# Block 1's standard deviation on ScalarE, block 2's statistics beside it, and the d mask later: a spectral mixer with a token MLP

## The chip, the cores and the metric

The kernel runs on one core of a Trainium2 chip. A core has five engines that run side by side and meet through semaphores: TensorE (PE) for matrix products, VectorE (DVE) and ScalarE (ACT) for element-wise work, GpSimd (POOL) for small operations and gathers, and SyncE (SP), whose queue issues most transfers (DMAs) between main memory and the core. Each engine works through its own list of instructions in order: an instruction that waits holds up all that stand behind it on that engine. The metric is the device time of one execution in microseconds (us), the median over several executions.

## The reference

Two branches work on the same 2048 tokens of 512 channels and are mixed by a gate per token.

```
g = sigmoid((x * gate_w).sum(-1, keepdims=True))
a = irfft2(rfft2(x) * (w_r + 1j*w_i))              # spectral branch, over tokens and channels
h = layernorm(x_B)                                 # over the channels
u = gelu(einsum("bsd,sf->bdf", h, w1) + b1)        # token MLP, 2048 -> 1792
b = transpose(einsum("bdf,fs->bds", u, w2) + b2)   # 1792 -> 2048
out = g * a + (1 - g) * b
```

The kernel takes one tensor x for both branches (`A_x`). All inputs and the output are bf16.

## The kernel before, in words

The 2048 tokens are 16 blocks of 128. The MLP's first product contracts over tokens, so it takes one block after another: `mm1(b, ft)` multiplies the weights of block b for one slice of 128 hidden features with the normalized block `hn[:, b]` and accumulates in PSUM. Eight feature slices (ft 0 to 7) are accumulated at the same time, so every block feeds eight matmuls of 512 columns, and PE can begin with block 0 as soon as that block is normalized. Blocks 0 to 11 go through in this order; then each slice takes blocks 12 to 15 and is passed to a gelu. The six other slices (`products`, line 459, weights `w1b`) and the whole second product (line 469, weights `w2t`) come later, as filling work between the matmuls of the spectral branch.

The front of the kernel is therefore a pipeline. SP's queue loads tokens (`load_x`, line 90, tiles `xa` and `xb`) and weights (`load_w1a`, line 93) in small pieces and in turn. DVE makes the statistics of a block (`bstat`, line 246) and aggregates them (line 253, or 297 for block 0). Then there are three ways to the normalized block:

- Block 0: ACT takes the square root of the variance plus epsilon (line 298), DVE the reciprocal (line 300) and the normalization (line 271). ACT needs its table for square roots for this, loaded by line 289; the later sines need another table, loaded by line 306.
- Blocks 1 to 5 (`NDVE` is 6): DVE adds epsilon (line 255), POOL raises to the power -0.5 (line 258), DVE normalizes (line 271).
- Blocks 6 to 15, in pairs: POOL makes the power; mean times that is formed on DVE (line 264, pairs 6/7 and 14/15) or POOL (line 262, the others); ACT normalizes (line 267).

DVE's order is written out by hand (the schedule is manual): the statistics of the next block stand between epsilon and the normalization of this block.

Beside this, the kernel makes the matrices of its Fourier transforms. DVE makes integer angles `md` for the d axis (line 291) and reduces them with a bit mask (line 195, function `mask`); ACT takes sines and cosines of them into `TD` (`sines_d`, lines 198 and 201). The same happens for the token axis: `ma`, `mc` made by ACT (lines 308 and 309), masked by DVE, sines into `TA`. SP's queue later transposes TD and TA into TI and TB (lines 347 and 349).

After that the spectral branch runs on DVE and PE: sums and differences of token blocks on DVE (`YA`, `YB`), token transforms (lines 514 to 518) and d transforms (line 526) on PE, the spectral weights on DVE (`PMA` and `PMB`, lines 533 to 563), the inverse on PE (lines 652 to 674, evacuated by ACT in line 630), and the last sums on DVE. Where PE's transforms stand among the filling matmuls is decided when the program is built, by a planner: `clock` starts at a given time and moves on by 0.2165 us for each filling matmul, and `fill_to(T)` issues filling matmuls until `clock` reaches a written due time (`T_TA`, `T_TB`, `T_IA`, `T_IB`, `T_Y`). The finished y blocks of the second product are evacuated by ACT (line 449).

Of the kernel before, what the change touches and what calls it, by code (L numbers as in the profile page):

```python
# [8 lines left out]
ActF = mybir.ActivationFunctionType  # L9
# [11 lines left out]
NFT = 14  # L21
FT1 = 8
NDVE = 6
# [20 lines left out]
def kernel(  # L44
# [13 lines left out]
    nc = tc.nc  # L58
# [9 lines left out]
    def H(i, shape, name, dt=BF16):  # L68
        return big.tile(shape, dt, tag=f"h{i}", name=name)
# [7 lines left out]
    def bank(name):  # L77
        return psum.tile([P, 512], F32, tag="mm", name=name, bufs=2)
# [10 lines left out]
    def load_x(b0, b1):  # L89
        nc.sync.dma_start(out=xh[b0 // 8][:, b0 % 8:(b1 - 1) % 8 + 1], in_=xv[:, b0:b1])  # L90

    def load_w1a(b0, b1):
        nc.sync.dma_start(out=w1a[b0 // 4][:, b0 % 4:(b1 - 1) % 4 + 1], in_=w1v[:, b0:b1, 0:FT1 * P])
# [28 lines left out]
    load_w1a(0, 1)  # L122
    load_x(1, 2)
    for b in range(1, 3):
        load_w1a(b, b + 1)
        load_x(b + 1, b + 2)
    load_x(4, 6)
    load_w1a(3, 4)
    load_x(6, 8)
# [16 lines left out]
    consts = small.tile([P, 6], F32, name="consts")  # L146
# [47 lines left out]
    def mask(m, n):  # L194
        nc.vector.tensor_single_scalar(m, m, n - 1, op=Alu.bitwise_and)

    def nsin(dst, m, n):
        nc.scalar.activation(dst, m, ActF.Sin, bias=c_mpi, scale=2.0 * PI_IN / n)

    def psin(dst, m, n):  # L200
        nc.scalar.activation(dst, m, ActF.Sin, bias=c_pi, scale=-2.0 * PI_IN / n)

    md = H(6, [P, 2, 3, P], "md", I32)
# [3 lines left out]
    def sines_d():  # L207
        nsin(TD[:, :, 1], md[:, 1], 1024)
        nsin(TD[:, :, 2], md[:, 0], 1024)
        psin(TD[:, :, 0], md[:, 0], 1024)  # L210

    def angles_a(v):
        mask(ma[v][:], 2048)
        if v == 0:
            mask(mc[:], 2048)

    def sines_a(v):
        if v == 1:
            nsin(TA[:, :, 1], ma[1][:], 2048)
        else:  # L220
            nsin(TA[:, :, 2], ma[0][:], 2048)
            psin(TA[:, :, 0], ma[0][:], 2048)
            nsin(TA[:, 0, 2, 0:1], mc[:], 2048)
            psin(TA[:, 0, 0, 0:1], mc[:], 2048)


    stats = small.tile([P, NB, nc.vector.BN_STATS_DIM], F32, name="stats")
    mv = small.tile([P, NB, nc.vector.BN_AGGR_DIM], F32, name="mv")
    rstd = small.tile([P, NB], F32, name="rstd")
# [6 lines left out]
    pb = bank("pb")  # L236
# [8 lines left out]
    def bstat(b):  # L245
        nc.vector.bn_stats(out=stats[:, b, :], in_=xh[b // 8][:, b % 8, :])  # L246

    def on_dve(b):
        return b <= NDVE or b == NB - 2

    def aggr(b0, b1):
        for b in range(b0, b1):
            nc.vector.bn_aggr(out=mv[:, b, :], in_=stats[:, b, :])
        eng = nc.vector if on_dve(b0) else nc.gpsimd
        eng.tensor_scalar(mv[:, b0:b1, 1], mv[:, b0:b1, 1], 1e-5, 0.0, op0=Alu.add, op1=Alu.add)  # L255
        if not on_dve(b0):
            nc.gpsimd.tensor_scalar(nmr[:, b0:b1], mv[:, b0:b1, 0], -1.0, 0.0, op0=Alu.mult, op1=Alu.add)
        nc.gpsimd.tensor_tensor(rstd[:, b0:b1], mv[:, b0:b1, 1], c_mhalf.to_broadcast([P, b1 - b0]), op=Alu.pow)  # L258

    def norm(b0, b1):  # L260
        if not on_dve(b0):
            nc.gpsimd.tensor_mul(nmr[:, b0:b1], nmr[:, b0:b1], rstd[:, b0:b1])  # L262
        else:
            nc.vector.scalar_tensor_tensor(nmr[:, b0:b1], mv[:, b0:b1, 0], -1.0, rstd[:, b0:b1],
                                           op0=Alu.mult, op1=Alu.mult)
        for b in range(b0, b1):
            nc.scalar.activation(hn[:, b, :], xh[b // 8][:, b % 8, :], ActF.Identity,  # L267
                                 bias=nmr[:, b:b + 1], scale=rstd[:, b:b + 1])

    def norm_dve(b):  # L270
        nc.vector.tensor_scalar(hn[:, b, :], xh[0][:, b, :], mv[:, b, 0:1], rstd[:, b:b + 1],  # L271
                                op0=Alu.subtract, op1=Alu.mult)
# [20 lines left out]

    bcol = small.tile([P, NFT + NB], F32, name="bcol")
    b1f, b2f = bcol[:, 0:NFT], bcol[:, NFT:]
    bstat(0)
    nc.vector.bn_aggr(out=mv[:, 0, :], in_=stats[:, 0, :])
    nc.scalar.activation(rstd[:, 0:1], mv[:, 0, 1:2], ActF.Sqrt, bias=consts[:, 5:6], scale=1.0)
    nc.scalar.copy(b1f, pb[:, 0:NFT])
    nc.vector.reciprocal(rstd[:, 0:1], rstd[:, 0:1])  # L300
    norm_dve(0)
    bstat(1)
    aggr(1, 2)
    norm_dve(1)
    bstat(2)
    nc.scalar.activation(sink[:], consts[:, 2:3], ActF.Sin, bias=c_mpi, scale=0.0)
    for v in range(2):
        nc.scalar.activation(ma[v][:], krow[:], ActF.Identity, bias=consts[:, 3 + v:4 + v], scale=acol[:, 0:1])
# [4 lines left out]
    for b in range(2, NDVE):  # L313
        bstat(b + 1)
        norm_dve(b)
        if b == 2:
            mask(md[:], 1024)
            sines_d()
        if b + 1 < NDVE:
            aggr(b + 1, b + 2)  # L320
    for b in range(NDVE, NB, 2):
        if b > NDVE:
            bstat(b)
        if b == NDVE + 2:
            norm(b - 2, b)
        bstat(b + 1)
        aggr(b, b + 2)
        if b == NB - 2:
            angles_a(1)
        if b > NDVE:  # L330
            norm(b, b + 2)
        if b == NB - 6:
            angles_a(0)
            sines_a(0)
# [4 lines left out]
    for q in range(4):  # L339
# [8 lines left out]
                                in_=TD[:].rearrange("p s t k -> p (s t k)"))  # L348
    nc.sync.dma_start_transpose(out=TB[:].rearrange("p s t k -> p (s t) k"),
                                in_=TA[:].rearrange("p s t k -> p (s t k)"))  # L350
# [132 lines left out]
    def hook(b):  # L483
        store(b)

    clock = [32.8]
    act = [0.0]

    def fill(n):
# [306 lines left out]
    b = NB - 1  # L796
# [36 lines left out]
```

## Time and profile before

| what | value |
|---|---|
| median of 3 runs | 129.39 us (129.38 to 129.5) |
| the profiled execution, own time | 129.24 us |
| its span, first to last instruction | 127.5 us |
| PE busy | 121.4 us, 95% |
| DVE busy | 111.5 us, 87% |
| ACT busy | 89.5 us, 70% |
| POOL busy | 40.9 us, 32% |
| granted TensorE clock | 0.999 |
| chain that ended last, by engine | PE 81%, DVE 6%, ACT 4%, POOL 3%, DMA 2%, issue 1% |
| moved by DMA | 24.05 MB |

The span covers only the instructions; the execution's own time is 1.74 us longer. A row of the time order gives start, duration, engine, line, operation, the tile written and the tiles read, and in brackets the idle time just before it with what ended it. The chain that ended last is found by going back from the last instruction, at each step to what released it. "busy" says how long an engine worked, not whether its work was on the path that sets the end.

### The profile page before, as it was taken

To read this page: it belongs to the slowest core of one execution; us is meant where nothing else is said; L and a number is where in the kernel's file an instruction comes from. 1 tells how busy PE (TensorE), PEld (TensorE's weight loads), DVE (VectorE), ACT (ScalarE), POOL (GpSimd) and SP (SyncE) were. 2 spreads that over 40 slices of the span, in tenths; PEclk is the share of its full clock that TensorE was granted. 3 is DMA by queue.
4 is the path that set the end of the run, shared out by engine and by line. 5 is a ranking of instruction groups with operands and counts; after the bars stand their busy time and mean duration, and the time that the engine had idled before them with its cause. 6 is when DMAs were issued, how large, how long until landed. Compare 5 with 4: busy or idle time off the path is not lost.

```text
span 127.5 us, 2061 instructions
## 1 busy us (share of the span) xinstructions
PE 121.4 (95%) x737; PEld 65.1 (51%) x750; DVE 111.5 (87%) x190; ACT 89.5 (70%) x136; POOL 40.9 (32%) x68
## 2 busy tenths in 40 slices
PE   6989999999999999999999999999999999999980
PEld 2334434444444576557764766467644444444570
DVE  4699998999999999999999999999999999992140
ACT  4774159999897799999994599339785599422410
POOL 7314378999843699300140000000000000250300
PEclk9999999999999999999999999999999999999999
DMA  3899999997899999999689205810021101279991
GB/s 100 279 314 367 375 377 351 292 309 249 206 224 161 306 290 292 291 278 296 153 234 292 50 0 154 261 42 0 0 75 53 41 5 49 72 86 197 184 211 29
DMA packets 34635, 24.05 MB, mean 189 GB/s; under 512 B 5536, under 2 KB 32032, under 8 KB 34624
## 3 DMA queue, kind: packets, MB, share of 16 engines
q1 hardware_dynamic: 32516, 21.02, 60.6%
q0 software_dynamic: 1936, 2.76, 12.5%
q8 instruction: 6, 0.10, 0.3%
q10 hardware_dynamic: 172, 0.13, 0.3%
q14 instruction: 5, 0.04, 0.1%
HBM read 19.15 MB, written 3.67 MB: 179 GB/s over the span
## 4 chain that ended last, share of the span: by engine, by line
PE 81%; DVE 6%; ACT 4%; POOL 3%; DMA 2%; issue 1%
PE yb L469 34%; PE u L459 16%; PE u L275 14%; PE ivt L658 4%; PE dp L526 3%; POOL rstd L258 3%; PE tok L517 3%; PE yb L801 2%; PE tok L518 2%; PE ivd L674 2%; DVE stats L246 2%; DVE hn L271 2%; DMA xa<-in_A_x_dram 2%; ACT R L630 2%; DVE mv L255 1%
## 5 line engine op out<-in xcount | busy, mean ns | idle before, releaser
L469 PE MATMUL yb<-gl,w2t 128*128 128x512 bf16 x203 | 46.4, 379 | 0.4
L469 PEld LDWEIGHTS <-w2t 128*128 128x128 bf16 x210 | 20.2, 98 | 22.0
L275 PE MATMUL u<-hn,w1a 128*128 128x512 bf16 x126 | 28.3, 379 | 0.9 <-DVE hn L271 0.4
L459 PE MATMUL u<-hn,w1b 128*128 128x512 bf16 x92 | 22.6, 379 | 0.2
L449 ACT ACTIVATE tbv<-yb,ombb,omg 128x512 bf16<-128x512 f32 x15 | 11.7, 778 | 13.5 <-PE yb L469 13.5
L275 PEld LDWEIGHTS <-w1a 128*128 128x128 bf16 x128 | 12.5, 98 | 16.6 <-issue 2.2
L779 POOL DMA_DIRECT2D out_dram<-ap x3 | 4.0, 1528 | 49.5 <-DVE ap L774 45.3
L459 PEld LDWEIGHTS <-w1b 128*128 128x128 bf16 x96 | 9.0, 98 | 8.0
L630 ACT CAST R<-ivt 128x1024 bf16<-128x1024 f32 x8 | 7.8, 1037 | 4.9 <-PE ivt L658 4.9
L286 ACT ACTIVATE junk<-prod 128x512 bf16<-128x512 bf16 x16 | 10.1, 630 | 0.3
L355 ACT ACTIVATE gl<-u,bcol 128x512 bf16<-128x512 f32 x14 | 9.2, 688 | 1.3 <-PE u L459 0.8
L258 POOL TENSOR_TENSOR rstd<-mv,consts 128x1 f32<-128x1 f32 (+1 forms) x10 | 6.7, 666 | 8.2 <-DVE mv L255 8.1
L630 ACT CAST H<-ivd 128x1024 bf16<-128x1024 f32 x7 | 6.8, 1026 | 0.8 <-PE ivd L674 0.8
L267 ACT ACTIVATE hn<-xb,nmr,rstd 128x512 bf16<-128x512 bf16 x8 | 5.9, 802 | 1.3 <-POOL nmr L262 1.3
L788 DVE TENSOR_TENSOR tbv<-tbv,ap 128x512 bf16<-128x512 bf16 x3 | 1.3, 426 | 5.6 <-ACT tbv L449 5.6
L246 DVE BATCH_NORM_STATS2 stats<-xa 128x6 f32<-128x512 bf16 x8 | 5.5, 686 | 0.4 <-DMA xa<-in_A_x_dram 0.4
L548 DVE TENSOR_TENSOR tatb<-PMA,wn 128x1024 bf16<-128x1024 bf16 x8 | 5.0, 690 | 0.2 <-PE tok L518 0.2
L246 DVE BATCH_NORM_STATS2 stats<-xb 128x6 f32<-128x512 bf16 x8 | 5.2, 676 | 0.0
L674 PEld LDWEIGHTS <-R 128*128 128x128 bf16 x64 | 3.9, 98 | 2.2 <-ACT R L630 2.2
L548 DVE TENSOR_TENSOR tatb<-PMB,wn 128x2048 bf16<-128x2048 bf16 x4 | 4.7, 1227 | 0.2
L674 PE MATMUL ivd<-TI,R 128*128 128x128 bf16 x64 | 4.9, 219 | 0.0
L519 ACT CAST ZA<-tok 128x1024 bf16<-128x1024 f32 x4 | 4.0, 1018 | 1.2 <-PE tok L518 1.1
(198 smaller groups left out, 222.7 us busy)
## 6 DMA issues: line engine op xcount, KB each, us to landing
w2t<-in_B_w_dram SPq DMA_DIRECT2D x8, 896.0 KB
w1b<-in_B_w_dram SPq DMA_DIRECT2D x3, 1024.0 KB
w1a<-in_B_w_dram SPq DMA_DIRECT2D x2, 1024.0 KB
out_dram<-tbv SPq DMA_DIRECT2D x14, 128.0 KB
out_dram<-ap POOLq DMA_DIRECT2D x3, 512.0 KB, 6.9
w1a<-in_B_w_dram SPq DMA_DIRECT2D x4, 256.0 KB
w1a<-in_B_w_dram SPq DMA_DIRECT2D x2, 512.0 KB
xb<-in_A_x_dram SPq DMA_DIRECT2D x2, 512.0 KB
```

What stands on the lines that cost most here:

```text
L246: nc.vector.bn_stats(out=stats[:, b, :], in_=xh[b // 8][:, b % 8, :])
L258: nc.gpsimd.tensor_tensor(rstd[:, b0:b1], mv[:, b0:b1, 1], c_mhalf.to_broadcast([P, b1 - b0]), op=Alu.pow)
L267: nc.scalar.activation(hn[:, b, :], xh[b // 8][:, b % 8, :], ActF.Identity, bias=nmr[:, b:b + 1], scale=rstd[:, b:b + 1])
L275: nc.tensor.matmul(u1[ft], lhsT=w1a[b // 4][:, b % 4, ft * P:(ft + 1) * P], rhs=hn[:, b, :], start=(b == 0), stop=(b == NB - 1))
L286: nc.scalar.activation(junk[:], prod[b // 8][:, b % 8], ActF.Copy, accum_out=glog[:, b:b + 1])
L355: nc.scalar.activation(gl[:, ft, :], src, ActF.Gelu_apprx_tanh, bias=b1f[:, ft:ft + 1], scale=1.0)
L449: nc.scalar.activation(tbv[0][:, b], y[:], ActF.Identity, bias=gate["ombb2"][:, b:b + 1], scale=gate["omg"][:, b:b + 1])
L459: nc.tensor.matmul(u[:], lhsT=w1b[c][:, b, k * P:(k + 1) * P], rhs=hn[:, b, :], start=(b == 0), stop=(b == NB - 1))
L469: nc.tensor.matmul(y[:], lhsT=w2t[b // 2][:, ft, (b % 2) * P:(b % 2 + 1) * P], rhs=gl[:, ft, :], start=(ft == 0), stop=(ft == NFT - 1))
L548: mul(tt[:, i, :, r:r + n], PM[:, 2 * s:2 * s + 2, r:r + n], w[:, None].to_broadcast([P, 2, n, 256]))
L630: nc.scalar.copy(out, pr[:].rearrange("p h n -> p (h n)"))
L674: nc.tensor.matmul(pr[:, c, o * P:(o + 1) * P], lhsT=plane(par, cos), rhs=TI[:, lst, t], start=True, stop=True)
```

## The change

Block 1 is handled as block 0 was: the square root on ACT, the reciprocal on DVE, without the epsilon operation and POOL's power. The statistics of block 2 stand between the aggregate and the reciprocal of block 1 on DVE. The tokens of blocks 2 and 3 are issued ahead of the weights of blocks 1 and 2 on SP's queue. The mask of the d angles moves on DVE from behind the normalization of block 2 to behind the aggregates of blocks 6 and 7; the d sines move on ACT from ahead of the normalization of block 6 to behind that of block 7. The planner's clock starts at 32.6 instead of 32.8. In the built program this puts one more filling matmul ahead of the transforms on PE and moves a few evacuations on ACT: that of the second y block (line 449) stands ahead of the first two evacuations of the inverse instead of behind them.

```diff
     load_w1a(0, 1)
     load_x(1, 2)
     for b in range(1, 3):
+        load_x(b + 1, b + 2)
         load_w1a(b, b + 1)
-        load_x(b + 1, b + 2)
     load_x(4, 6)
...
-    bstat(0)
-    nc.vector.bn_aggr(out=mv[:, 0, :], in_=stats[:, 0, :])
-    nc.scalar.activation(rstd[:, 0:1], mv[:, 0, 1:2], ActF.Sqrt, bias=consts[:, 5:6], scale=1.0)
-    nc.scalar.copy(b1f, pb[:, 0:NFT])
-    nc.vector.reciprocal(rstd[:, 0:1], rstd[:, 0:1])
-    norm_dve(0)
-    bstat(1)
-    aggr(1, 2)
-    norm_dve(1)
-    bstat(2)
+    for b in range(2):
+        bstat(b)
+        nc.vector.bn_aggr(out=mv[:, b, :], in_=stats[:, b, :])
+        nc.scalar.activation(rstd[:, b:b + 1], mv[:, b, 1:2], ActF.Sqrt, bias=consts[:, 5:6], scale=1.0)
+        if b == 0:
+            nc.scalar.copy(b1f, pb[:, 0:NFT])
+        else:
+            bstat(2)
+        nc.vector.reciprocal(rstd[:, b:b + 1], rstd[:, b:b + 1])
+        norm_dve(b)
     nc.scalar.activation(sink[:], consts[:, 2:3], ActF.Sin, bias=c_mpi, scale=0.0)
...
     for b in range(2, NDVE):
         bstat(b + 1)
         norm_dve(b)
-        if b == 2:
-            mask(md[:], 1024)
-            sines_d()
         if b + 1 < NDVE:
             aggr(b + 1, b + 2)
     for b in range(NDVE, NB, 2):
         if b > NDVE:
             bstat(b)
         if b == NDVE + 2:
             norm(b - 2, b)
+            sines_d()
         bstat(b + 1)
         aggr(b, b + 2)
+        if b == NDVE:
+            mask(md[:], 1024)
         if b == NB - 2:
             angles_a(1)
...
-    clock = [32.8]
+    clock = [32.6]
     act = [0.0]
```

## The prediction

> **What bounds the kernel now.** I read the engine shares first, then the chain that ended last, then the order in time of each engine up to 25 us, and last the meeting points of TensorE (PE) and VectorE (DVE) further on. The page:
>
> ```profile
> span 127.5 us, 2061 instructions
> PE 121.4 (95%) x737; PEld 65.1 (51%) x750; DVE 111.5 (87%) x190; ACT 89.5 (70%) x136; POOL 40.9 (32%) x68
> ```
>
> PE has 6 us of idle time, so the gain has to be found in its gaps. PE's order in time shows where they are:
>
> ```profile
> 4.78 1.89 PE L275 MATMUL u<-hn,w1a 128*128 128x512 bf16 x8
> 6.90 1.89 PE L275 MATMUL u<-hn,w1a 128*128 128x512 bf16 x8 [0.23 <-DVE hn L271]
> 9.00 7.16 PE L275 MATMUL u<-hn,w1a 128*128 128x512 bf16 x31 [0.21 <-DVE hn L271]
> 16.37 17.43 PE L275 MATMUL u<-hn,w1a 128*128 128x512 bf16 x79 [0.21 <-ACT hn L267]
> ...
> 70.54 1.92 PE L658 MATMUL ivt<-TB,PMA 128*128 128x256 bf16 x16
> ...
> 74.72 0.39 PE L469 MATMUL yb<-gl,w2t 128*128 128x512 bf16 x1
> 75.18 1.03 PE L658 MATMUL ivt<-TB,PMA 128*128 128x256 bf16 x8
> ```
>
> The pace comes from the tail: ACT evacuates one y block every 3.02 us there (114.81, 117.83), 14 matmuls of 512 columns each, so 0.2156 us a matmul. (Counts in such rows run short where a record is missing.) One block of the first product is 8 of them, 1.725 us. Block 0 starts at 4.78, so six blocks without gaps would end at 15.13; block 6 starts at 16.37. That is 1.24 us of gaps, made of 0.395 before block 1 (6.90 against 6.505), 0.375 before block 2, 0.09 before block 3 (its weight loads go on at 10.82, against 10.725) and 0.375 before block 6. After 16.37 I find one gap worth naming: at 74.94 PE should go on and does at 75.18, 0.24 us.
>
> What PE waits for is a round trip on DVE and GpSimd (POOL), block after block (chain of waits, in order of time):
>
> ```profile
> 5.36 0.19 DVE mv L253
> ...
> 5.58 0.16 DVE mv L255
> ...
> 5.82 0.59 POOL rstd L258
> ...
> 6.44 0.41 DVE hn L271
> ...
> 8.95 0.47 DVE md L195
> ...
> 15.31 0.17 DVE nmr L264
> ```
>
> DVE is nearly as tight as PE: from 22.50 to 115 its order in time has hardly a gap, and it delivers PMA at 70.48 (L558) and PMB at 83.94, where PE arrives at 70.53 and 84.06. So an earlier PE is worth something only if DVE comes earlier by as much.
>
> **The change, part by part.** All times are those of the one profiled execution (span 127.5, own time 129.24 us, 0.15 below the median of 129.39); I shift them.
>
> *Block 1 by ScalarE (ACT), block 2's statistics under it.* Block 0 is unchanged: its normalized block ends at 4.73 and the block 1 statistics run until 5.33, the aggregate from 5.36 to 5.54. ACT did copy b1f by 4.48 and is free: root 5.58 to 5.87 (0.29, row of L298). DVE meanwhile runs the block 2 statistics, 5.45 to 6.14, and can start the reciprocal at 6.06 (0.61 between starts, as at 13.39 to 14.00). From reciprocal to normalization is 0.20 (4.12 to 4.32): 6.26 instead of 6.44. PE starts block 1 at 6.72 instead of 6.90: 0.18 gained. Two waits are added: DVE waits for tokens 2 with the reciprocal behind, and ACT's sine table load moves from 4.50 to about 5.9, with the four angle operations behind it, done by 10.1 instead of 8.53; their reader, the mask of ma0 at 17.60, hides that.
>
> *Block 2* loses the statistics (0.69) from its path. Aggregate 6.59, epsilon 6.80, power 7.03 to 7.61, normalization 7.64 instead of 8.54, ending at 8.05. PE ends block 1 at 8.445: the gap is gone and block 2 starts there, 0.555 earlier.
>
> *The d mask leaves the path of block 3.* Blocks 4 and 5 show the plain pitch, 10.36, 11.71, 13.06: 1.35. So normalization 3, 4, 5 at 8.99, 10.34, 11.69, 1.37 earlier each. PE needs them at 10.17, 11.90, 13.62: covered by over 0.7.
>
> *The mask in its new place* stands between the pair 6, 7 and the statistics of block 8. The epsilon of the pair moves from 14.33 to 12.96, the mask starts at 13.04 and adds 0.47; statistics 8 then allow the L264 step at 14.12. The power beside it would start at 13.21. These rows say what a POOL operation costs beside such a mask:
>
> ```profile
> 14.58 0.70 POOL L258 TENSOR_TENSOR rstd<-mv,consts 128x2 f32<-128x2 f32 x1 [1.55 <-DVE mv L255]
> ...
> 17.66 0.65 POOL L262 TENSOR_TENSOR nmr<-nmr,rstd 128x2 f32<-128x2 f32 x1
> ...
> 19.63 0.20 POOL L262 TENSOR_TENSOR nmr<-nmr,rstd 128x2 f32<-128x2 f32 x1
> ...
> 21.40 1.07 POOL L258 TENSOR_TENSOR rstd<-mv,consts 128x2 f32<-128x2 f32 x1
> ```
>
> The two long ones run beside the masks of 17.60 and 21.23: 0.37 and 0.45 more. I take 0.37, the same operation: power until 14.28, L264 at 14.31, 1.00 earlier than 15.31. Without the collision it would be 14.12, 1.19 earlier; with 0.45 it is 0.92. L264 to PE is 1.06 (15.31 to 16.37), so block 6 could start at 15.37, and PE is free at 15.345. PE gains 1.00 here, DVE also 1.00, and every later step of DVE stands behind it.
>
> The Trainium skill, page "SBUF — State Buffer", section "SBUF: two separate sides", says that a VectorE operation using two ports locks GpSimd out for its whole length, the loser starting about 115 ns after its end. By that the power would run 13.70 to 14.40 and the sum would lose another 0.12; the two rows above agree with a full block and are what the sum uses.
>
> *The d sines* (1.63 from 9.45 to 11.08) go between ACT's blocks 7 and 8: hn 6 at 14.51, hn 7 until 16.03, sines until 17.58, hn 8 until 18.3. PE needs it at 18.8: covered, with 0.5 left. The last hn goes from 26.65 to about 25.8, needed at 26.37; the a sines, the gelu table and the gelus follow 0.85 earlier than now, with two banks free over 1 us before PE wants them. The transpose of TD is issued at 31.05, long after.
>
> *Tokens 2 and 3 before the weights of blocks 1 and 2* on SP's queue: same issues, one slot (0.47) exchanged each. Landing of loads for which nobody waited isn't shown, so I use bytes moved: 0.78 MB by 5.0 us, 1.08 by 6.0, 1.58 by 7.5, 5.35 by 18.0, plus 0.4 as with the first tokens (0.13 MB moved by 2.4, consumer at 2.85). Tokens 2 then land by 4.7 (needed 5.45), weights 1 by 5.9 (their first weight load 6.3), tokens 4 and 5 by 7.9 (needed 8.24), weights 4 and 5 by 11.2 (11.7), weights 8 to 11 by 18.1 (18.6). All covered, the closest by 0.3. Upper ends by who reads them now without a wait: tokens 2 at 6.77, tokens 4 at 9.61, weights 4 at 12.3. The cost lies between 0 and a full loss of the gain; I take 0, as the bytes are nearest to a measurement of landing.
>
> *Clock 32.8 to 32.6* puts one more matmul (0.2156) before each transform. PE reaches PMA at 70.53 - 1.00 + 0.22 = 69.75 with DVE done at 69.48, and PMB at about 83.1 (all gains counted) with DVE done at 82.94. No new wait, and none to spare. It also completes y block 1 before the inverse instead of two matmuls after. ACT's rows say what that does:
>
> ```profile
> 71.62 1.93 ACT L630 CAST R<-ivt 128x1024 bf16<-128x1024 f32 x2 [2.85 <-PE ivt L658]
> 73.43 0.79 ACT L449 ACTIVATE tbv<-yb,ombb,omg 128x512 bf16<-128x512 f32 x1
> 74.11 1.94 ACT L630 CAST H<-ivd 128x1024 bf16<-128x1024 f32 x2
> ```
>
> L449 now stands between the R and H evacuations; afterwards it runs before the first R, while ACT waits for PE, so H comes 0.68 earlier and the 0.24 gap at 75.18 closes. Next late is R0: ACT's evacuations follow at 0.91, so R0 ends 5.72 after the first inverse matmul and PE wants it at about 5.67. From the first inverse matmul to the d product of R0 it is 6.59 now with 10 y matmuls; then 5.77 with 7, which is 5.77 + 3 x 0.2156 = 6.42: 0.17 gained. Ends: 0 and 0.24.
>
> The sum: 1.00 in front + 0.17 in the inverse = 1.17 us; the end after PE's last matmul (stores) moves along. 129.24 - 1.17 = 128.07 for the profiled execution, 128.2 as a median.
>
> **Rivals.**
> A, data come later than the bytes say, and DVE or PE waits in front: if tokens 4 and 5 land at 8.9 instead of 7.9, statistics 4 and all of DVE behind lose 0.66, block 6 with them, and 0.5 is left: 128.9. For it: DMA runs at 280 to 400 GB/s throughout, without slack. Against: the margins above. The Trainium skill ("DMA: Bandwidth & Descriptors", section "Queues, rings and completion order") says that completions of one queue need not come in order of issue, which would favour A; no row here shows it. 0.18.
> B, slower: tokens 2 land late and the reciprocal of block 1, behind their statistics, waits. Landing at t gives normalization at t + 0.81 and PE block 1 at t + 1.27. PE reaches block 6 later than 16.37 when block 1 starts after 7.74, that is t > 6.47; at t = 6.77 (the upper end) it is 8.04, 0.30 late, less 0.17: 129.5; at 7.0 it is 129.75. Against: 0.66 MB suffice, moved by 4.4 us. 0.08, with anything else of that sign, 0.10.
> C, no change: PE comes earlier but DVE doesn't, so PE waits at PMA or PMB for what it gained, 129.3. It needs a new DVE stall of about 1 us ahead of 70; the only DVE waits after 15.4 there are POOL's power at 21.92 (0.58), which moves along, and 0.19 at 60.1. 0.05.
> D, more: POOL doesn't collide, the 0.24 gap closes wholly and the small gaps of 0.05 in PE's chain shrink: 127.8. 0.07.
>
> **How the numbers follow.** Forecast 0.60, own range 127.95 to 128.5 (collision 0.37 or 0.45, inverse 0 to 0.24, DMA margins). A 0.18, B 0.10, C 0.05, D 0.07. Range 127.7 to 129.0: it holds the forecast, D and most of A, and leaves out B and C. Within 0.2% (0.26 us) is what a measurement of this kernel can't tell from no change. Faster 0.85 (forecast, A, D), same 0.05, slower 0.10.
>
> **What would show it.** Right: PE block 1 near 6.7, block 2 without gap near 8.45, block 6 near 15.4; the power of 6, 7 at about 1.07; DVE's nmr at 14.3 and prod near 21.6; PMA at 69.5; no gap between the last R of block 1 and the fourth inverse product; PE's end near 122.8. Wrong: DVE's statistics of block 2 or 4 idle for tokens, weight loads idle at block 1, 4 or 8, hn 8 later than 18.8, or PE idle before PMB for more than 0.3.

## The result and the profile after

| | kernel before | changed kernel |
|---|---|---|
| median, 20 runs each | 129.41 us | 128.89 us |
| the profiled execution, own time / span | 129.24 / 127.5 us | 128.94 / 127.2 us |

The ratio is 0.9953, with a 95% interval of 0.9934 to 0.9972. That is 0.61 us less (0.36 to 0.85); by the medians it is 0.52. 1.17 us less had been forecast: the sign was right, the gain came out at half. Two of the 20 executions of the changed kernel took 131.8 us, in a slower state; the ratio leaves them out.

The first lines of the page of the changed kernel, and from its chain of work that ended last the shares by engine and two of its longest pieces (start, length, what):

```profile
span 127.2 us, 2074 instructions
PE 122.1 (96%) x750; PEld 65.1 (51%) x750; DVE 111.4 (88%) x190; ACT 89.6 (70%) x137; POOL 39.3 (31%) x67
...
PE 91%; DMA 3%; DVE 1%; SPq 1%; issue 0%
```

```profile
2.13 4.10 DMA xa<-in_A_x_dram
7.51 26.06 PE u L275 x120
```

ACT and POOL, 4% and 3% of the chain before, have left it, and DVE went from 6% to 1%: the round trips are gone. What stands at the head now is a transfer of 4.10 us, one block of tokens. PE's order in time, the rows that answer to those shown of before (the last row of a view is cut off where its window ends, so its count can run short):

```profile
4.84 2.23 PE L275 MATMUL u<-hn,w1a 128*128 128x512 bf16 x8
7.51 26.06 PE L275 MATMUL u<-hn,w1a 128*128 128x512 bf16 x120 [0.44 <-DVE hn L271]
33.41 3.62 PE L459 MATMUL u<-hn,w1b 128*128 128x512 bf16 x16
...
70.52 1.91 PE L658 MATMUL ivt<-TB,PMA 128*128 128x256 bf16 x16
...
74.70 1.05 PE L658 MATMUL ivt<-TB,PMA 128*128 128x256 bf16 x8
...
83.96 1.91 PE L658 MATMUL ivt<-TB,PMB 128*128 128x256 bf16 x16
...
120.33 3.25 PE L801 MATMUL yb<-gl,w2t 128*128 128x256 bf16 x42
```

In the kernel before, the rows that answer to three of these:

```profile
33.64 3.62 PE L459 MATMUL u<-hn,w1b 128*128 128x512 bf16 x15
...
84.07 1.91 PE L658 MATMUL ivt<-TB,PMB 128*128 128x256 bf16 x16
...
120.65 3.25 PE L801 MATMUL yb<-gl,w2t 128*128 128x256 bf16 x42
```

From block 1 to block 15 there is no gap left, but block 1 starts at 7.51, 0.61 later than before (6.90), where 0.18 earlier was forecast. Five blocks of 1.725 us then bring block 6 at 16.135 instead of 16.37: 0.235 gained of the 1.00 forecast. DVE's order says why block 1 is late:

```profile
4.38 0.41 DVE L271 TENSOR_SCALAR hn<-xa,mv,rstd 128x512 bf16<-128x512 bf16 x1
4.71 0.68 DVE L246 BATCH_NORM_STATS2 stats<-xa 128x6 f32<-128x512 bf16 x1
5.42 0.18 DVE L298 BATCH_NORM_AGGREGATE mv<-stats 128x2 f32<-128x6 f32 x1
6.25 0.69 DVE L246 BATCH_NORM_STATS2 stats<-xa 128x6 f32<-128x512 bf16 x1 [0.65 <-DMA xa<-in_A_x_dram]
6.87 0.15 DVE L304 RECIPROCAL rstd<-rstd 128x1 f32<-128x1 f32 x1
7.05 0.41 DVE L271 TENSOR_SCALAR hn<-xa,mv,rstd 128x512 bf16<-128x512 bf16 x1
```

The statistics of block 2 wait 0.65 us for tokens 2, and behind them stand the reciprocal and the normalization of block 1, whose root ACT finished long before. PE's weight loads (PEld, one ahead of each matmul) show that the weights of block 1 were late too, though less:

```profile
6.93 0.10 PEld L275 LDWEIGHTS <-w1a 128*128 128x128 bf16 x1 [0.36 <-DMA w1a<-in_B_w_dram]
```

The six other slices of the first product (line 459, weights `w1b`; "second product slices" in one of the expectations) begin 0.23 earlier than before (33.41 against 33.64). One more filling matmul (0.2156) stands ahead of the inverse, so the inverse starts 0.02 earlier (70.52 against 70.54); the way from its first to its second product takes 13.44 us instead of 13.53; and one filling matmul fewer is left behind it. Together PE's last group starts 0.32 earlier (120.33 against 120.65), which is the 0.30 between the two profiled executions. The medians show 0.2 more, because the execution profiled of the kernel before lay 0.17 below its median and this one 0.05 above.

### The profile page after: what moved, and what is told of

It is laid out like the page before. It is cut to its first block, busy times and chain, and to the rows that moved or that the text cites. A ratio compares the mean times of both kernels' runs of the same rounds, so it can differ in the third digit from the quotient of the medians.

```text
span 127.2 us, 2074 instructions
## 1 busy us (share of the span) xinstructions
PE 122.1 (96%) x750; PEld 65.1 (51%) x750; DVE 111.4 (88%) x190; ACT 89.6 (70%) x137; POOL 39.3 (31%) x67
## 4 chain that ended last, share of the span: by engine, by line
PE 91%; DMA 3%; DVE 1%; SPq 1%; issue 0%
PE yb L469 36%; PE u L275 20%; PE u L459 16%; PE ivt L658 5%; DMA xa<-in_A_x_dram 3%; PE ivd L674 3%; PE dp L526 3%; PE yb L801 2%; PE tok L517 2%; PE tok L518 2%; SPq L90 1%; DVE stats L246 1%; PE ivt L652 0%; PE tok L514 0%; SPq L93 0%; DVE hn L271 0%
## 5 line engine op out<-in xcount | busy, mean ns | idle before, releaser
L469 PE MATMUL yb<-gl,w2t 128*128 128x512 bf16 x210 | 47.5, 379 | 0.0
L459 PE MATMUL u<-hn,w1b 128*128 128x512 bf16 x96 | 23.3, 379 | 0.0
L449 ACT ACTIVATE tbv<-yb,ombb,omg 128x512 bf16<-128x512 f32 x15 | 11.6, 775 | 15.6 <-PE yb L469 15.6
L258 POOL TENSOR_TENSOR rstd<-mv,consts 128x2 f32<-128x2 f32 (+1 forms) x9 | 6.3, 703 | 8.2 <-DVE mv L255 8.1
L267 ACT ACTIVATE hn<-xa,nmr,rstd 128x512 bf16<-128x512 bf16 x2 | 1.5, 806 | 5.2 <-DVE nmr L264 5.2
```

The costliest lines, as they stand in the source:

```text
L449: nc.scalar.activation(tbv[0][:, b], y[:], ActF.Identity, bias=gate["ombb2"][:, b:b + 1], scale=gate["omg"][:, b:b + 1])
L459: nc.tensor.matmul(u[:], lhsT=w1b[c][:, b, k * P:(k + 1) * P], rhs=hn[:, b, :], start=(b == 0), stop=(b == NB - 1))
L469: nc.tensor.matmul(y[:], lhsT=w2t[b // 2][:, ft, (b % 2) * P:(b % 2 + 1) * P], rhs=gl[:, ft, :], start=(ft == 0), stop=(ft == NFT - 1))
```

## The experiments

Two accounts compete for the missing half. T: the steps of the engines are worth what was forecast, and loads that land later than their bytes suggest take half of it away. Against it: the sum of the engines' steps itself was wrong (the mask and the planner's clock give nothing, or DVE and PE lose it again later). A third term, PE's own slow start, turned up only in these runs, with the tokens on ACT's queue. All ratios are to the kernel before, on the same chip.

**The old order of the loads, everything else as changed.**

```diff
     for b in range(1, 3):
+        load_w1a(b, b + 1)
         load_x(b + 1, b + 2)
-        load_w1a(b, b + 1)
```

> The changed kernel, with the tokens of blocks 2 and 3 issued behind the weights of blocks 1 and 2 again, as before the change. Theory T (block 1 waits for tokens 2, whose landing follows their issue by some 4.1 us): tokens 2 are issued 0.47 later (2.60) and land near 6.7, normalization 1 at 7.5, PE starts block 1 near 7.95 and block 6 near 16.6; time 129.3, 0.45 slower than the changed kernel. Rival R (landing follows the bytes in flight, whose sum up to tokens 2 and weights 1 is the same in either order): tokens 2 again near 6.2 to 6.4, PE block 1 near 7.5 to 7.7, 128.9 to 129.0.

Measured: 129.40 against 129.47, ratio 0.9993 (0.9976 to 1.0009). The gain is gone: the interval lies wholly above that of the changed kernel. DVE's and PE's order of its profile:

```profile
6.97 0.69 DVE L246 BATCH_NORM_STATS2 stats<-xa 128x6 f32<-128x512 bf16 x1 [1.32 <-DMA xa<-in_A_x_dram]
...
8.22 26.06 PE L275 MATMUL u<-hn,w1a 128*128 128x512 bf16 x118 [0.52 <-DVE hn L271]
```

Tokens 2 land 0.72 later than in the changed kernel (0.47 was expected), and PE's block 1 starts 0.71 later, one for one. This execution took 130.56 us, 1.16 over its median (its weight loads also wait 1.02 us for `w1b` at 54), so it shows the mechanism and not its usual size; the median shows that.

**The statistics of block 2 behind the normalization of block 1.**

```diff
-        else:
-            bstat(2)
         nc.vector.reciprocal(rstd[:, b:b + 1], rstd[:, b:b + 1])
         norm_dve(b)
+    bstat(2)
```

> The changed kernel, with the statistics of block 2 behind the normalization of block 1, so that block 1 does not wait for tokens 2. Theory T: normalization 1 near 6.3; then weights 1, which landed near 6.9 in the changed kernel, set PE block 1 near 7.0 instead of 7.5; block 2 normalized near 8.25, block 6 near 15.85 instead of 16.13; 128.6, 0.25 faster than the changed kernel. Rival R (the wait is not what limits): the statistics now stand on the path of block 2 again, 0.6 there, and the time is 128.9 or more.

Measured: 128.81, ratio 0.9946 (0.9926 to 0.9966), not to be told from the changed kernel; the 0.25 us expected don't show. In its profile block 1 is normalized at 6.14 without a wait, block 2 at 8.27, and PE's last group starts at 120.08, 0.25 earlier than in the changed kernel's. Putting the statistics first buys block 2 time (7.64 forecast against 8.27) but stakes block 1 on the landing of tokens 2; in the times the two come out even.

**Only block 1's root on ACT**: the kernel before, with these lines instead of POOL's power for block 1; loads, mask and clock are the old ones.

```diff
-    bstat(0)
-    nc.vector.bn_aggr(out=mv[:, 0, :], in_=stats[:, 0, :])
-    nc.scalar.activation(rstd[:, 0:1], mv[:, 0, 1:2], ActF.Sqrt, bias=consts[:, 5:6], scale=1.0)
-    nc.scalar.copy(b1f, pb[:, 0:NFT])
-    nc.vector.reciprocal(rstd[:, 0:1], rstd[:, 0:1])
-    norm_dve(0)
-    bstat(1)
-    aggr(1, 2)
-    norm_dve(1)
+    for b in range(2):
+        bstat(b)
+        nc.vector.bn_aggr(out=mv[:, b, :], in_=stats[:, b, :])
+        nc.scalar.activation(rstd[:, b:b + 1], mv[:, b, 1:2], ActF.Sqrt, bias=consts[:, 5:6], scale=1.0)
+        if b == 0:
+            nc.scalar.copy(b1f, pb[:, 0:NFT])
+        nc.vector.reciprocal(rstd[:, b:b + 1], rstd[:, b:b + 1])
+        norm_dve(b)
     bstat(2)
```

> The kernel before the change with one part alone: block 1's root on ACT and its reciprocal on DVE; statistics of block 2 behind its normalization, old order of loads, old place of mask and sines, clock 32.8. Theory T (that part does not depend on tokens 2): normalization 1 near 6.2 instead of 6.44, block 2's near 8.3 instead of 8.54, block 6 on PE near 16.1 instead of 16.37: 129.1 to 129.2. Rival R: block 0's slow matmuls end after 6.6 anyway and weights 1 land late, nothing gained: 129.4.

Measured: 129.52, ratio 0.9997 (0.9972 to 1.0022): worth nothing alone, where some gain was expected. Block 1 is normalized at 6.14, as expected, but DVE then only waits for the same tokens:

```profile
7.08 0.69 DVE L246 BATCH_NORM_STATS2 stats<-xa 128x6 f32<-128x512 bf16 x1 [0.52 <-DMA xa<-in_A_x_dram]
...
8.88 0.41 DVE L271 TENSOR_SCALAR hn<-xa,mv,rstd 128x512 bf16<-128x512 bf16 x1
```

Block 2 is normalized at 8.88, later than the 8.54 of before. Nor could PE have taken block 1 much before the 6.90 of the kernel before: in this execution its weight loads reach their short spacing only at 5.62, so that block 0 ends at about 6.91 (5.62 + 6 x 0.2156). In this profile, then, a faster root needs earlier tokens and a quick block 0 to be worth something.

**Half of the bytes of the weights `w1a`**, in the changed kernel and in the kernel before alike. This takes traffic away from the front and leaves every instruction of the engines in place; four of the eight slices are multiplied by the weights of the other four, so the output is not that of the reference.

```diff
-        nc.sync.dma_start(out=w1a[b0 // 4][:, b0 % 4:(b1 - 1) % 4 + 1], in_=w1v[:, b0:b1, 0:FT1 * P])
+        nc.sync.dma_start(out=w1a[b0 // 4][:, b0 % 4:(b1 - 1) % 4 + 1, 0:4 * P], in_=w1v[:, b0:b1, 0:4 * P])
...
-        nc.tensor.matmul(u1[ft], lhsT=w1a[b // 4][:, b % 4, ft * P:(ft + 1) * P], rhs=hn[:, b, :],
+        nc.tensor.matmul(u1[ft], lhsT=w1a[b // 4][:, b % 4, (ft % 4) * P:(ft % 4 + 1) * P], rhs=hn[:, b, :],
```

> The changed kernel with only half of the w1a weights loaded (512 of 1024 columns; slices 4 to 7 multiply by the weights of slices 0 to 3 again, so the matmuls and weight loads on PE are as many, the bytes of the front 2 MiB fewer and the output another). Theory T (landing of tokens and weights holds back the front): tokens 2 land by 5.5, no weight load waits, and what is left is PE's slow clock in block 0 (up to 0.2 a matmul); second product slices start near 32.7 to 33.1 instead of 33.4; time 127.9 to 128.3. Rival R (the landing follows the issue, 4.1 us behind it, whatever the bytes): tokens 2 near 6.2 as before, 128.7 to 128.9.

> The kernel before the change with the same half of the weights left out. Theory T: its front waited for no load (only for its own chain of power and normalization), so it stays at 129.2 to 129.4, and the change, with data in time, is worth about 1.0 to 1.2 as the prediction's sum had it. Rival R (before also is held by data): it comes down by as much as the changed kernel does with half the weights, and the difference of the two stays near 0.5.

Measured: 128.31 (ratio 0.9914, 0.9883 to 0.9944) for the changed kernel, 129.25 (0.9983, 0.9961 to 1.0006) for the kernel before. Between the two lie 0.94 us by the medians; the ratio of the ratios is 0.9931, 0.89 us, give or take some 0.5 by the two intervals. That holds the 1.17 of the forecast, but also the 0.61 of the full kernels: that loads take something away is shown by the waits in the profiles, not by these times alone. The profile of the changed kernel with half the bytes is that of the fastest of its eight executions (127.70 us, 0.61 below their median), so its rows show the front with hardly anything late. They agree closely with the forecast. DVE and PE:

```profile
6.19 0.41 DVE L271 TENSOR_SCALAR hn<-xa,mv,rstd 128x512 bf16<-128x512 bf16 x1
...
7.58 0.41 DVE L271 TENSOR_SCALAR hn<-xa,mv,rstd 128x512 bf16<-128x512 bf16 x1
...
14.14 0.16 DVE L264 SCALAR_TENSOR_TENSOR nmr<-mv,rstd 128x2 f32<-128x2 f32 x1
```

```profile
4.75 27.97 PE L275 MATMUL u<-hn,w1a 128*128 128x512 bf16 x126
32.56 2.75 PE L459 MATMUL u<-hn,w1b 128*128 128x512 bf16 x12
...
69.67 1.91 PE L658 MATMUL ivt<-TB,PMA 128*128 128x256 bf16 x16
...
83.11 1.91 PE L658 MATMUL ivt<-TB,PMB 128*128 128x256 bf16 x16
...
119.48 3.25 PE L801 MATMUL yb<-gl,w2t 128*128 128x256 bf16 x42
```

The forecast had 6.26, 7.64, 14.31, PMA at 69.75 and PMB at 83.1. With half the bytes the kernel before looks as it did with all of them:

```profile
16.34 17.43 PE L275 MATMUL u<-hn,w1a 128*128 128x512 bf16 x79 [0.20 <-ACT hn L267]
...
120.64 3.25 PE L801 MATMUL yb<-gl,w2t 128*128 128x256 bf16 x42
```

So 120.64 - 119.48 = 1.16 us: in this execution the sum of the engines' steps came out, and the waits for tokens 2 and weights 1 are gone. By the medians 0.94 of it is there. Tokens 2, issued at 2.13 as before, are used at 5.43 without a wait, 3.3 us after their issue; in the changed kernel's profile 4.10 passed, so the landing is no fixed time behind the issue. The kernel before had the gaps of its round trip in any case, and late data fell into them; the change took the gaps away and left the data.

**The d mask and sines in their old place**, with all the bytes and with half of them.

```diff
         norm_dve(b)
+        if b == 2:
+            mask(md[:], 1024)
+            sines_d()
...
             norm(b - 2, b)
-            sines_d()
...
-        if b == NDVE:
-            mask(md[:], 1024)
```

> The changed kernel, with the d mask and the d sines where they were before. Theory T (the mask stands ahead of block 6's L264 on DVE in either place, so moving it takes nothing off the path but the overlap with the power): L264 near 15.2 instead of 15.0, PE block 6 near 16.3 instead of 16.13, 129.0, within 0.2 of the changed kernel. Rival R, the prediction's reading that the move takes 0.47 off the path of blocks 3 to 5 and so of PE: 129.3 or more.

> The changed kernel with half of the w1a weights left out (slices 4 to 7 take those of slices 0 to 3 again) and the d mask and the d sines in their old place. Theory T (with data in time too, the mask is ahead of block 6 in either place and blocks 3 to 5 have slack): normalizations 3 to 5 are 0.47 later, L264 within 0.15 of the 14.14 of the run with half the weights, time within 0.15 of its 128.3. Rival R, the reading that the mask was on the path of PE: 0.4 slower, 128.7.

Measured: 128.74, ratio 0.9942 (0.9921 to 0.9962) with all the bytes, as the changed kernel; with half of them 128.38, ratio 0.9923 (0.9908 to 0.9938), against 128.31 and 0.9914. So moving the mask is worth nothing that can be measured, as T says. With half the bytes and the mask in its old place the normalizations 3 to 5 come at 9.51, 10.87 and 12.22, some 0.56 later, of which 0.10 is the later start of this execution (block 1 is normalized at 6.29 against 6.19) and the rest the mask. PE has them covered: its blocks run in one piece from 4.85. The L264 step comes at 14.46 instead of 14.14, more than the 0.15 later that was expected, and block 6 pays a little for it: its first weight load stands at 15.53, with 0.26 us idle before it where some 0.12 is usual. The `w1b` slices start at 32.79, 0.23 later than with the mask moved, which is about the 0.10 of the start and the 0.14 at block 6.

With all the bytes PE's weight loads show the next late data:

```profile
12.47 6.59 PEld L275 LDWEIGHTS <-w1a 128*128 128x128 bf16 x32 [0.53 <-DMA w1a<-in_B_w_dram]
```

The weights of block 4 (counted from 0) were forecast for 11.2. Those of block 8, forecast for 18.1, come at 19.53.

**Tokens 2 on ACT's queue**, behind the small `brow` load, instead of SP's.

```diff
-    def load_x(b0, b1):
-        nc.sync.dma_start(
+    def load_x(b0, b1, eng=None):
+        (eng or nc.sync).dma_start(
...
-    for b in range(1, 3):
-        load_x(b + 1, b + 2)
-        load_w1a(b, b + 1)
+    load_x(2, 3, nc.scalar)
+    load_w1a(1, 2)
+    load_x(3, 4)
+    load_w1a(2, 3)
```

> The changed kernel, with tokens 2 issued on ACT's queue behind the b1 row (near 1.4 us) instead of SP's (2.1 us), so that every later load on SP's queue is issued 0.47 earlier. Theory T: tokens 2 land near 5.4, normalization 1 at 6.3, weights 1 (issued at 2.13) by 6.4, PE block 1 near 6.75, block 6 near 15.4 to 15.6; 128.2 to 128.4. Rival R (bytes in flight decide, not the issue): tokens 2 still near 6.2, 128.9.

Measured: 128.55, ratio 0.9933 (0.9908 to 0.9958), between the two accounts of the expectation. DVE does not wait for tokens 2, and PE's view lists no gap from block 0 on:

```profile
5.65 0.66 DVE L247 BATCH_NORM_STATS2 stats<-xa 128x6 f32<-128x512 bf16 x1
...
4.78 28.52 PE L276 MATMUL u<-hn,w1a 128*128 128x512 bf16 x126
33.13 2.11 PE L460 MATMUL u<-hn,w1b 128*128 128x512 bf16 x9
```

Yet the `w1b` slices start at 33.13, not at the 32.56 of the run with half the bytes, with nearly the same start (4.78 against 4.75) and no gap listed in either. The 0.57 us lie in block 0 itself. PE's weight loads there are spaced 0.38 to 0.43 apart until 6.37, and 0.22 after:

```profile
5.16 0.15 PEld L276 LDWEIGHTS <-w1a 128*128 128x128 bf16 x1 [0.28 <-issue]
5.58 0.15 PEld L276 LDWEIGHTS <-w1a 128*128 128x128 bf16 x1 [0.27 <-issue]
6.01 0.15 PEld L276 LDWEIGHTS <-w1a 128*128 128x128 bf16 x1 [0.28 <-issue]
6.37 3.55 PEld L276 LDWEIGHTS <-w1a 128*128 128x128 bf16 x17 [0.21 <-issue]
```

Four matmuls took 1.59 us (4.78 to 6.37) where four at 0.2156 take 0.86: 0.73 lost. With half the bytes the short spacing began at 5.01, so that run was quick here as well.

This was the slowest of the six executions (129.14 us), though PE's last group starts at 120.05, earlier than the 120.33 of the changed kernel: what follows that group took 7.15 us to the end of the span, against 6.87. And a new load is late: the statistics of block 1 start 0.51 us behind the start of block 0's normalization, where 0.33 is usual. In the two profiles of the next version it is 0.62 and 0.77, and there the wait is put down to tokens 1.

**The same, with the weights of blocks 4 to 5 and 8 to 11 loaded in two pieces each**, and later once more, beside the changed kernel again.

```diff
-    load_w1a(4, 6)
+    load_w1a(4, 5)
+    load_w1a(5, 6)
...
-    load_w1a(8, 12)
+    load_w1a(8, 10)
+    load_w1a(10, 12)
```

> The kernel with tokens 2 on ACT's queue, and weights 4/5 and 8 to 11 loaded in two transfers each instead of one. Theory T (a weight load of block 4 or 8 waits until the whole transfer of two or four blocks has landed, as the 0.53 and 0.47 at 12.47 and 19.53 in the run with the mask put back): no weight load waits for a transfer; 128.2 to 128.4, 0.1 to 0.3 faster than with tokens 2 on ACT's queue alone. Rival R: the waits are rare or hidden, two more issues on SP (0.47 each) delay what follows: 128.55 or more.

> The changed kernel once more, beside the following three on the same chip. Theory T (its front depends on when tokens 2 and the first weights land, which differs from run to run, and on how long PE's clock stays slow in block 0): 128.7 to 128.9; in the profile either a wait for tokens 2 or a full block 0 at a slow clock. Rival R (a constant): the same 0.65 of waiting at 5.6 us as in the first profile.

> The kernel with tokens 2 on ACT's queue and the weights of blocks 4/5 and 8 to 11 in two transfers each, once more beside the changed kernel. Theory T: 0.2 to 0.35 faster than the changed kernel on the same chip, no wait of DVE for tokens 2. Rival R: what the first run showed was the chip's difference; same as the changed kernel within 0.1.

Measured: 128.58, ratio 0.9927 (0.9900 to 0.9953), where 128.2 to 128.4 was expected; again, on another chip, 128.42, ratio 0.9924 (0.9899 to 0.9948), beside 128.57, ratio 0.9945 (0.9925 to 0.9965) for the changed kernel. That is the best time of a kernel that keeps all its weights, by 0.15 us (medians) or 0.27 us (ratios) better than the changed kernel; the intervals overlap, so it isn't shown to be better, and still less whether the split adds to it.

The changed kernel's second profile (128.56 us) is the more telling one. It is the same program, and this time other loads are late:

```profile
5.55 0.66 DVE L246 BATCH_NORM_STATS2 stats<-xa 128x6 f32<-128x512 bf16 x1
...
8.91 0.69 DVE L246 BATCH_NORM_STATS2 stats<-xa 128x6 f32<-128x512 bf16 x1 [0.51 <-DMA xa<-in_A_x_dram]
```

Tokens 2 are there by 5.55 (6.23 the first time), and tokens 4, which cost nothing in the first profile, come at 8.91. Both are within the upper ends of the forecast; tokens 4 are a full 1.0 us later than their bytes said.

**The planner's clock back at 32.8.**

```diff
-    clock = [32.6]
+    clock = [32.8]
```

> The changed kernel with the planner's clock at 32.8 again. Theory T (the 32.6 puts one y evacuation ahead of the inverse's first ones and closes the 0.24 gap of PE there; 0.09 came of it in the profile, where 0.17 was predicted): 0.05 to 0.2 slower than the changed kernel. Rival R: with DVE earlier by only 0.3, the matmul less ahead of the inverse makes PE wait for PMA or PMB: 0.3 slower.

Measured: 128.98, ratio 0.9958 (0.9938 to 0.9978), beside 0.9945 on the same chip: 0.17 us by the ratios, 0.41 by the medians, with intervals that overlap. The inverse is as it was in the kernel before: from its first product to the fourth 71.46 to 76.10, 4.64 us, against 4.18 in the changed kernel (70.52 to 74.70), though with one filling matmul more in it. Its profiled execution, at 130.15 us, has the latest tokens of all, tokens 4, past even the upper end of the forecast (9.61):

```profile
10.46 0.69 DVE L246 BATCH_NORM_STATS2 stats<-xa 128x6 f32<-128x512 bf16 x1 [2.01 <-DMA xa<-in_A_x_dram]
```

The clock can't have caused this: it is a constant of the plan behind the front, and the loads ahead of it are the same.

## Why the prediction was right in sign and wrong in size

**The failing step was "Tokens 2 and 3 before the weights of blocks 1 and 2".** It put the landing of loads where their bytes are counted as moved, plus 0.4, and took a cost of 0 between bounds of 0 and a full loss. Counting bytes put tokens 2 at 4.7, weights 1 at 5.9, weights 4 at 11.2, tokens 4 at 7.9. They were first used, after a wait, at 6.25 and 6.93 in the first profile of the changed kernel, at 12.47 with the mask back, and at 8.91 and 10.46 in the two further profiles. In the changed kernel's own profile 0.65 MB, all that stands up to tokens 2 on SP's queue, had been moved by about 4.4 us (0.58 MB by 4.0, 0.75 by 5.0), and tokens 2 were usable 1.8 us later. Nor do the bytes tell one run from the other: by 8.0 us 1.64 MB had been moved where tokens 4 came at 8.91, and 1.66 MB where they came at 10.46. The count says how much is under way, not which of the loads is complete. The 0.4 was calibrated on the first tokens, the first load of its queue. The mean of the two bounds would have been nearer than the end that I took. The upper ends were not safe either: besides tokens 4 at 10.46, the weights of block 4 came at 12.47 and 13.31 (12.3 had been the end), and with the old order of loads tokens 2 at 6.97 and 7.08 (6.77).

The landing is not all of it. In the first profile the `w1b` slices start 0.77 later than forecast (33.41 against 33.64 - 1.00). Of this 0.58 is the wait for tokens 2: block 1 starts at 7.51, and at 6.93 its first weights were there. The other 0.19 belongs to those weights and to two slow matmuls of block 0, which ends at about 6.91 where block 1 was to start at 6.72. With tokens 2 on ACT's queue the wait is gone, and the slices still start 0.49 late, by four slow matmuls: 0.73, less the 0.215 that PE was to wait ahead of block 1 anyway. **The sum had no term for PE's slow start.** How the two share the missing half in the medians is not shown.

**The front, 1.00.** Its mechanism was right: with data in time the normalizations come at 6.19, 7.58, 8.95, 10.30 and 11.66 (forecast 6.26, 7.64, 8.99, 10.34, 11.69), block 6 joins without a gap, and the `w1b` slices start 1.05 earlier (33.61 against 32.56). With all the bytes 0.23 of it was left in one profile and 0.62 in the other (33.02 against 33.64). At PE's last group the two are 0.32 and 0.71 ahead of the kernel before (120.33 and 119.94 against 120.65); the medians and the ratio, 0.52 and 0.61, lie in this span.

**"The d mask leaves the path of block 3"** is true of DVE's order and worth nothing that the times show, for the reason that the same paragraph gives, cover of over 0.7 at blocks 3 to 5. Block 6 pays for the mask in the new place nearly as in the old: the mask delays the power there by collision (0.94 instead of 0.70), in the old place by standing ahead of it. At L264 the move gained 0.22 in the profiles with half the bytes (14.14 against 14.46, less 0.10 of later start), and PE about 0.14 of it.

**The collision of POOL's power with the mask**, forecast 0.37: it is 0.24. The power of pair 6, 7 took 0.94 instead of 0.70, beside a mask that runs from 13.86 to 14.41:

```profile
14.03 0.94 POOL L258 TENSOR_TENSOR rstd<-mv,consts 128x2 f32<-128x2 f32 x1 [1.55 <-DVE mv L255]
```

It ended at 14.97. By the row that the prediction took it would have been 15.10; but that row stood beside a mask of 1024 elements a partition (0.69 us) and this mask has 768 (0.55), which is about the difference. By the Trainium skill ("SBUF — State Buffer", "SBUF: two separate sides"), with a full block until the mask's end and the start 0.115 after it, an estimate is 15.22. The two rows of before don't agree with a full block either, as the prediction had read them: by it they would have ended at 18.57 and 22.73 (masks until 18.26 and 21.92), and they ended at 18.31 and 22.47. All three ended some 0.26 sooner than a full block allows.

**The inverse, 0.17** with ends 0 and 0.24: 0.09 measured from its first to its second product (13.53 to 13.44), with all the bytes and with half of them alike. The L449 evacuation does stand ahead of the first R, as forecast:

```profile
70.73 0.78 ACT L449 ACTIVATE tbv<-yb,ombb,omg 128x512 bf16<-128x512 f32 x1 [2.19 <-PE yb L469]
71.60 1.93 ACT L630 CAST R<-ivt 128x1024 bf16<-128x1024 f32 x2
73.41 1.95 ACT L630 CAST H<-ivd 128x1024 bf16<-128x1024 f32 x2
```

and no new wait shows at PMA or PMB.

**The rivals.** A gave 128.9, and 128.89 came. Its mechanism, data later than their bytes with DVE waiting, is the right one, but in the first profile DVE waited at tokens 2, which is B's place, and only in the second at tokens 4, which is A's; that the number fits to 0.01 is luck. The range, 127.7 to 129.0, holds the result only by A's share; the forecast's own range, 127.95 to 128.5, doesn't. B's arithmetic held to the hundredth: with t = 6.25 it gives normalization 1 at 7.06 and PE's block 1 at 7.52, and 7.05 and 7.51 were seen. Its point of decision, t > 6.47, was not reached in any of the profiles with the new order of loads, and was passed with the old order (6.97), whose gain was gone. C did not happen: DVE reaches PMA 0.37 earlier (L558 ends at 70.11 against 70.48), and PE finds it ready. D did not happen.

What stays open: why the same load lands at 5.5 in one execution and at 6.2 in another, and how large the part of the planner's clock is by itself. Nor do I account for what follows PE's last group, which took 6.30 us in one profile of the split version and 7.21 in the other: that spread alone is larger than the gain.

## What to carry to other kernels

A wait that is removed in front of a saturated stretch of loads uncovers the next one; in the front here that was a landing, and behind it PE's slow start. Where a reader waited, the bytes moved had put the landing 1.0 to 2.6 us too early: take them as a lower end. The time at which a reader takes a load today without a wait is a better price, but no upper bound (9.61 for tokens 4, 10.46 in one run). Put an instruction that needs late data behind, not ahead of, the work that does not; here, though, that order came out even. To separate engines from data, halve the bytes and leave the instructions: the fastest execution then matched the forecast to within 0.02 us in PE's order, and the medians gave 0.94 of 1.17.

## What had not been expected

PE's speed in block 0 differs from run to run, of the same program too (short spacing from 5.62 and from 5.25 in the two profiles of the changed kernel). It was busy from 0.98 us on in every run, yet the spacing of its weight loads drops from 0.38 to 0.43 us to 0.22 at 5.6 in the changed kernel, at 6.37 with tokens 2 on ACT's queue and at 6.89 with the old loads, and in the run with the planner's old clock its last warm-up matmul, before 4.5, already took 0.39 where it takes 0.61 in the run with tokens 2 on ACT's queue. That row and this:

```profile
4.09 0.39 PE L240 MATMUL pw<-warm 128*128 128x512 bf16 x1
```

```profile
4.20 0.61 PE L241 MATMUL pw<-warm 128*128 128x512 bf16 x1
```

That is a spread of over 2.5 us between runs, and each slow matmul costs about 0.2. The profile's row of the granted clock shows full speed in these slices, so the slow start has to be read from the spacing. The Trainium skill ("TensorE: Matmul & The Clock Gate", "What's actually happening") explains such a start by a window that runs freely, about 3.4 us long; it gives the end a variation of 500 ns either way, and a little further on 6 to 14 slow matmuls from run to run of one kernel. The spread here, most of such a window, fits the second and not the first, and the measurement decides. The kernel before had 0.395 us of slack ahead of block 1, which covered part of this; a kernel without gaps pays it in full (0.73 us in the run with tokens 2 on ACT's queue), and the sum of the prediction had no term for it.
